# Chunk-selected attention with a gated FFN: FFN products in free order with the first eight in parts, masks as minimum or select, unit 3 by DMA transposes

## The chip, the cores and the metric

The kernel runs on one core of a Trainium2 chip. The core has five engines with a queue each: TensorE (PE), VectorE (DVE), ScalarE (ACT), GpSimd (POOL) and SyncE (SP, which here only issues DMAs). The metric is the device time of one launch in microseconds, the median over runs.

## The reference, cut to what matters

```
ub     = sum_d max(q * k_min[chunk], q * k_max[chunk])      # 24 chunks of 32 keys
top    = the 6 chunks of largest ub among the causal ones, for each query
scores = q @ k.T / 8, kept where the chunk is in top and the key is not after the query
attn   = softmax(scores) @ v                                # 4 batches, 8 heads, 768 rows, 64 wide
x      = attn with the heads side by side                   # 3072 x 512
out    = (sigmoid(x @ w_gate) * (x @ w_val)) @ w_out        # d_ff 1536
```

All inputs and the output are float32.

## The kernel before, in words

The 24 blocks of 128 query rows (4 batches of 6) are cut into eight units of three blocks. Unit 0 holds the first block of batches 0, 1 and 2 (and the first block of batch 3 goes with unit 2): there every causal chunk is among the six, so no choice is made, and `first` (L604) does all of it. Units 1 to 7 go through `prepare` (L1263: keys and queries turned and cast, `choose` at L789 for the bounds and the choice), `attend` (L847: scores, exponential, causal mask, product with v, division) and a feed-forward part: `ffn` (L937) for units 0 to 3, and `ffn_pair` (L1016) for 4 with 5 and 6 with 7, where seven products do the work of eight.

The causal part of the mask lies in the diagonal blocks. `attend` and `first` clear the upper triangle of the exponentials with an `affine_select` on POOL (L880 and L658). The chunk mask is added in the score product itself: half of the 128 contracted rows hold the key, the other half a fixed pattern of -60000 (`hkp`, L498, copied from `epat`) against a 0/1 choice of the query (`hqm`). Values arrive in float32 and are cast to half precision on POOL (`cast_v`, L576; for the first blocks `vc`, L642, on POOL or ACT).

`finish` (L910) divides by the sum and turns x so that the FFN can contract over it. For units below XBAR = 4 this is done by TensorE (`xps`, L931) with an eviction (`xT`, L933); from unit 4 on it is a DMA transpose issued by SP (L920).

`ffn` runs for each of 12 blocks of 128 FFN columns a gate product `g` (4 matmuls of 384 columns, L956), a tanh on ACT, a value product `v` (L962) and a gating on DVE (`hg`, L964), and then the product with w_out (`project_out`, L968), which `o0`, `o1`, `o2` take in thirds of the 12 blocks for each of three row blocks. All `g`, `v` and `o` name the key "ffn" as written, so that they keep the order of the code among themselves.

The order of all work is written out: `ORDER` (L97 to L283) is one list of 1982 names, and each engine's queue is that list filtered by engine. After a colon stand the buffer slots that an operation takes, after an @ the engine where it is not the first that the operation allows. Every engine runs its queue strictly in order, so an operation that waits holds all that stand behind it on its engine. `Plan.add` (L50) finds what an operation depends on. The cost figures in `act`, `dve`, `pool` and `pe` (L286 to L302) are the planner's and have no effect on the program.

`BEATS` (L95) are transposes of a constant on TensorE with no use for the result, 78 of them in 13 groups. They stand between the first operations of the list. Loads are issued by SP, the weights by POOL (`weights`, L515), which casts them on the way; these wait for the operations `after0` to `after6` (L510), each of which reads a word of an earlier load.

Of the kernel before, what the change touches and what calls it, by code (L numbers as in the profile page):

```python
# [15 lines left out]
XBAR = 4  # L16
# [78 lines left out]
BEATS = (20, 9, 8, 3, 3, 10, 5, 1, 2, 2, 6, 6, 3)  # L95

ORDER = """  # L97
ident k3_u1:0 kcr0 epat0:0 kf1_0:0 v10 k0_u1 epat q2_u1 kf0_0 q1_u1 q0_u2:1 hkp010 hkp001@ACT k2_u1 ap0 hkp011@POOL
q3_u2 kn_u1_3:0 q0_u1 beat0:7 kT_u1_3:0 qf1_0:1 after2 kn_u1_0@POOL:1 qf0_0 kT_u1_0:1 k1_u1 qn_u1_1@DVE:0 hkp000 q3_u1
qT_u1_1:2 kt_u1_0:0 hkp100@POOL ident16 vf_0:2 kx0_u1_3 qf_u1_1:0 kt_u1_3@DVE:1 ap1 k0_u2 qn_u1_0:0 qn_u2_0@DVE:1  # L100
qf1_1:3 qn_u1_2@DVE:2 kn_u1_2:3 beat1:7 qT_u1_0:2 after0 kx1_u1_0:0 hkp110@ACT qT_u2_0:3 kf0_1:4 hk0_u1_3 qfT_0:4
kfT_0:5 kn_u1_1@POOL:1 qf16_0@DVE:0 qf0_1 qn_u2_3:4 kx1_u1_3 qn_u1_3:5 after3 vf_2:0 kf16_0:6 kxf0 hk1_u1_3@ACT
beat2:7 scf_0:0,4,1 v16_0_0 kT_u1_2:6 qf_u1_0 vf_1:1 kn_u2_0:0 hk0_u1_0 kx0_u1_2 hq0_u1_1@POOL expf_0_0 beat3:7
kT_u2_0:2 qT_u1_2:7 qf_u2_0:1 kf1_1 cmf_0_0 kt_u1_2:1 expf_0_1:2 q2_u2 hk1_u1_0@POOL beat4:0 pvf_0_0:3 kT_u1_1:0
qm_u1_1@ACT:0 hq1_u1_1@DVE kf0_2:0 qT_u1_3:4 after1 kx0_u1_0 vf1_2:1 qf0_2:1 kxf1:1 vc_2@ACT after6 qf1_2 qm_u1_0@ACT
kcr_f kx1_u1_2 cmf_0_1 kf1_2 qf_u1_2 kx1_u2_0:1 qf_u1_3 v11 beat5:1 pvf_0_1:7 k3_u2 qfT_1:6 kx0_u1_1 after4
qm_u1_3@ACT after5 wg0 kfT_1:4 q1_u2 rzf_0_1:0 kt_u2_0@DVE:0 qf16_1:5 k2_u2 hk0_u2_0 wv0 kt_u1_1:2 kf16_1@DVE:2 k1_u2
vf1_1:0 wg1 qm_u1_2 v_0_2:4 beat6:1 scf_1:4,6,1 qn_u2_2@DVE:3 hkp111 expf_1_1:3 v_0_3:3 beat7:1 qT_u2_2:5 qfT_2:1 hq0
vc_1@ACT kx1_u1_1 cmf_1_1 kfT_2:6 expf_1_0 rzf_0_0:1 kcr_u1@POOL xf_0_0:0 qf16_2:3 kf16_2@DVE:2 cmf_1_0 beat8:0
xpsf_0_0:3,0 xTf_0_0@ACT hkf0@DVE wv1 beat9:0 scf_2:6,1,2 qf_u2_2 xf_0_1:0 pvf_1_0:3 hk0_u1_2@ACT ub_u1:4,0 kx0_u2_0  # L110
hq0_u2_2@POOL expf_2_0 wg2 kn_u2_3@DVE:2 expf_2_1:1 hq0_u1_2@DVE pvf_1_1:6 rzf_1_0:0 hq0_u1_3 xf_1_0:1 cmf_2_1
ubn1_u1:0 qn_u2_1:0 vf1_3:3 rzf_1_1:0 hq1_u1_3 cmf_2_0 xf_1_1:2 beat10:5 qT_u2_1:0 xpsf_0_1:3 hq1 pvf_2_1:1
hq1_u2_0@POOL ubn0_u1 xpsf_1_1:6 xTf_0_1@ACT pvf_2_0:2 xpsf_1_0:7 kT_u2_3:5 hq0_u2_0 wv2 rzf_2_0:0 rzf_2_1:1
hk1_u2_0@ACT kn_u2_2@DVE:2 xf_2_0:1 wo0 qf_u2_1 v_0_1:0 xf_2_1:2 xTf_1_0@ACT beat11:4 xpsf_2_0:2 xTf_1_1@ACT ubm0_u1
xpsf_2_1:7 hk0_u1_1@ACT kn_u2_1@DVE:1 kT_u2_2:1 qT_u2_3:6 hk1_u1_1@POOL xTf_2_0 beat12:4 kT_u2_1:0 xTf_2_1 kt_u2_2:0
mx0_u1:0 wo1 hkp101@ACT g_u0_0:7,0,0 ap0_u1 wo2 apt0_u1:0 kx0_u2_2 qf_u2_3 v_u0_0:2 hq0_u1_0 hqm0_u1_2@DVE
g_u0_1:6,1,1 hq0_u2_3@POOL kx1_u2_1 hq1_u2_2@POOL v_u0_1:4 hk1_u1_2@POOL tanh_u0_1 tanh_u0_0 g_u0_2:3,2,2 hqm0_u1_0
hg_u0_1 kt_u2_1:1 v_u0_2:7 kx1_u2_2 hk0_u2_1@POOL tanh_u0_2 hg_u0_0 sc_u1_2_0:1,0 g_u0_3:3,1,3 hg_u0_2 exp_u1_2_0
# [187 lines left out]
def kernel(  # L306
# [1079 lines left out]
```

## Time and profile before

| | |
|---|---|
| median of 3 runs | 285.58 us (285.08 to 287.19) |
| profiled execution, whole | 284.64 us |
| its span, first to last instruction | 282.9 us |
| mean granted TensorE clock | 0.994 |
| bytes moved by DMA | 34.28 MB |
| first FFN product of unit 0 | 31.05 us |

The page gives each engine's busy time, the span in 40 slices, DMA queues, the chain of waits and the costliest groups of instructions. A row of a group reads: line, engine, operation, output from input, shape, count, then busy us and mean ns of one, then the idle time just before it and what ended it. In rows of the timeline the first two numbers are the start and the length in us.

### The profile page before, as it was taken

What the parts mean: (1) busy time and instruction counts of PE and PEld (TensorE: products, weight loads), DVE (VectorE), ACT (ScalarE), POOL (GpSimd) and SP (SyncE); (2) the same over time, 40 slices, a digit from 0 to 9 for tenths busy, and PEclk for the clock granted to TensorE, in tenths of its full rate; (3) what the DMA queues carried; (4) which work ended last, traced back from release to release, by engine and by line L of the source; (5) the groups of instructions that cost most, each with busy time, mean ns of one, the idle gap of its engine ahead of it and who ended that gap; (6) DMA issues with size and microseconds to landing.
All of it is one profiled execution on the core that took longest, in us unless ns stands there. A gap on an engine that the chain in (4) does not pass through costs nothing.

```text
span 282.9 us, 7408 instructions
## 1 busy us (share of the span) xinstructions
PE 271.4 (96%) x2746; PEld 187.4 (66%) x2746; DVE 245.1 (87%) x665; ACT 215.5 (76%) x467; POOL 144.5 (51%) x221
## 2 busy tenths in 40 slices
PE   6998899999999999999999999999999999999994
PEld 5875565765666656754777666667666786676783
DVE  2788778529979999997998998999999999999983
ACT  4787897665667956877899998989999937778620
POOL 7468673245433765773567974415648310347020
PEclk9799999999999999999999999999999999999999
DMA  6999999999989999999920112200001013010005
GB/s 174 292 232 184 197 197 208 162 189 222 147 194 163 228 173 215 180 205 185 228 62 17 30 30 67 89 20 13 14 16 29 16 49 117 0 39 37 3 19 204
DMA packets 130035, 34.28 MB, mean 121 GB/s; under 512 B 118096, under 2 KB 127056, under 8 KB 130000
## 3 DMA queue, kind: packets, MB, share of 16 engines
q1 hardware_dynamic: 125248, 29.11, 48.9%
q0 software_dynamic: 4752, 4.72, 10.2%
q8 instruction: 21, 0.34, 0.5%
q14 instruction: 14, 0.11, 0.1%
HBM read 30.67 MB, written 6.29 MB: 131 GB/s over the span
## 4 chain that ended last, share of the span: by engine, by line
PE 77%; DVE 12%; ACT 5%; issue 3%; POOL 2%; POOLq 0%; DVEq 0%; ACTq 0%
PE g_u L952 11%; PE v_u L952 11%; PE sc_u L863 10%; PE o_u L983 8%; PE pv_u L896 6%; PE suo_u6u L1210 3%; PE suv_u6u L1069 3%; PE suo_u4u L1210 3%; PE sug_u6u L1069 2%; PE sug_u4u L1069 2%; PE suv_u4u L1069 2%; PE ube_u L801 2%; PE sro_u6u L1210 1%; PE sro_u4u L1210 1%; PE srv_u6u L1069 1%
## 5 line engine op out<-in xcount | busy, mean ns | idle before, releaser
L874 ACT ACTIVATE att_u<-sc_u 128x512 f16<-128x512 f32 (+3 forms) x184 | 90.6, 550 | 14.1 <-PE sc_u L863 13.0
L880 POOL TENSOR_SCALAR_AFFINE_SELECT att_u<-att_u 128x384 f16<-128x384 f16 (+1 forms) x56 | 29.0, 529 | 40.0 <-ACT att_u L874 34.8
L952 PE MATMUL g_u<-xT_u,wg 128*128 128x384 f16 x192 | 39.0, 326 | 1.0 <-DVE hg_u L964 0.6
L952 PE MATMUL v_u<-xT_u,wv 128*128 128x384 f16 x192 | 39.0, 326 | 0.0
L983 PE MATMUL o_u<-wo,hg_u 128*128 128x512 f16 x144 | 36.1, 379 | 0.0
L960 ACT ACTIVATE gate_u<-g_u 128x384 f16<-128x384 f32 x48 | 23.1, 494 | 12.3 <-PE g_u L952 10.6
L964 DVE SCALAR_TENSOR_TENSOR hg_u<-gate_u,v_u 128x384 f16<-128x384 f16 x48 | 25.2, 537 | 5.4 <-PE v_u L952 4.2
L896 PEld LDWEIGHTS <-att_u 128*128 128x128 f16 x640 | 25.3, 98 | 4.7 <-issue 0.2
L863 PE MATMUL sc_u<-hqo,hko 128*128 128x128 f16 (+2 forms) x220 | 27.9, 243 | 0.3 <-ACT att_u L874 0.2
L863 PE MATMUL sc_u<-hqe,hke 128*128 128x128 f16 (+2 forms) x220 | 27.4, 243 | 0.3 <-DVE ubn_u L812 0.3
L896 PE MATMUL pv_u<-v,att_u 128*128 128x65 f16 x640 | 27.6, 193 | 0.0
L952 PEld LDWEIGHTS <-wg 128*128 128x128 f16 x192 | 18.2, 98 | 11.9 <-issue 1.4
L952 PEld LDWEIGHTS <-wv 128*128 128x128 f16 x192 | 18.3, 98 | 11.1 <-DVE x_u L915 0.3
L863 PEld LDWEIGHTS <-hko 128*128 128x128 f16 x220 | 17.0, 98 | 7.3 <-issue 1.6
L863 PEld LDWEIGHTS <-hke 128*128 128x128 f16 x220 | 16.3, 98 | 7.5 <-issue 1.5
L983 PEld LDWEIGHTS <-hg_u 128*128 128x128 f16 x144 | 13.2, 98 | 10.5
L578 POOL CAST v<-v 128x512 f16<-128x512 f32 x23 | 14.8, 659 | 2.6 <-DMA v<-in_v_dram 2.1
L915 DVE TENSOR_TENSOR x_u<-pv_u,rz_u 128x384 f16<-128x384 f32 (+1 forms) x28 | 14.7, 528 | 0.6
L1192 POOL TENSOR_TENSOR v<-hgp_u 128x384 f16<-128x384 f16 x5 | 4.5, 914 | 20.3 <-PE suv_u6u L1069 13.7
L473 PE MATMUL beat<-ident 128*128 128x128 f32 x78 | 13.4, 322 | 1.4 <-POOL ident masks.py:199 1.4
L824 DVE MAX8 mx_u<-ubn_u 128x8 f32<-128x8 f32 (+16 forms) x152 | 12.7, 157 | 0.0
L473 PEld LDWEIGHTS beat<-ident 128*128 128x128 f32 x78 | 11.3, 169 | 1.7 <-POOL ident masks.py:199 1.4
(284 smaller groups left out, 695.6 us busy)
## 6 DMA issues: line engine op xcount, KB each, us to landing
v<-in_v_dram SPq DMA_DIRECT2D x23, 256.0 KB, 4.6
k<-in_k_dram SPq DMA_DIRECT2D x12, 384.0 KB, 6.4
q<-in_q_dram SPq DMA_DIRECT2D x12, 384.0 KB, 5.8
out_dram<-osb_u SPq DMA_DIRECT2D x16, 256.0 KB, 2.8
wg<-in_moe_w_gate_dram POOLq DMA_DIRECT2D x3, 512.0 KB, 13.8
wv<-in_moe_w_val_dram POOLq DMA_DIRECT2D x3, 512.0 KB, 13.8
wo<-in_moe_w_out_dram POOLq DMA_DIRECT2D x3, 512.0 KB, 20.7
out_dram<-osb_u6u SPq DMA_DIRECT2D x5, 256.0 KB, 2.0
```

What stands on the lines that cost most here:

```text
L473: nc.tensor.transpose(at(beat), ident32, ident32)
L578: plan.add(f"v16_{b}_{ib}", {POOL: pool(H * D)}, lambda e: nc.gpsimd.tensor_copy(v16[b % 2][:, ib, :, 0:D], at(t)), reads=[t], writes=[("v ...
L863: nc.tensor.matmul(at(t)[:, o:o + 128 * m], hk[b % 2][e_][:, p, 128 * jb:128 * jb + 128], hq[u.side][e_][:, p, 128 * x:128 * (x + m)], sta ...
L874: plan.add(f"exp_{u.name}_{h}_{y}", {ACT: act(n)}, lambda e, t=t, att=att, b0=b0, n=n: nc.scalar.activation(at(att)[:, b0:b0 + n], at(t), ...
L880: nc.gpsimd.affine_select(out=dv, in_=dv, compare_op=ALU.is_ge, fill=0.0, base=0, pattern=[[0, u.m], [1, 128]], channel_multiplier=-1)
L896: nc.tensor.matmul(at(pv)[:, last, x, :], at(att)[:, c:c + 128], v16[b % 2][:, jb, h, :], start=(jb == 0), stop=(jb == ib))
L952: nc.tensor.matmul(at(t), w16[:, c, 128 * fb:128 * fb + 128], at(u.xt)[:, c, :], start=(c == 0), stop=(c == 3))
L960: plan.add(f"tanh_{u.name}_{fb}", {ACT: act(T)}, lambda e, g=g, gate=gate: nc.scalar.activation(at(gate), at(g), AF.Tanh, scale=0.5), read ...
L964: plan.add(f"hg_{u.name}_{fb}", {DVE: dve(T)}, lambda e, w_=w_, gate=gate, hg=hg: nc.vector.scalar_tensor_tensor(at(hg), at(gate), 1.0, at ...
L983: nc.tensor.matmul(at(o), hgs[c][1][1]()[:, 128 * tb:128 * tb + 128], wo16[:, fc, lo:hi], start=(c == 0), stop=(c == NFB - 1))
L1069: nc.tensor.matmul(at(t), left[i](c), right[i](c), start=first and c == 0, stop=c == 1, skip_group_check=not first)
L1210: nc.tensor.matmul(at(t), sums[what[i][0], f][1]()[:, 128 * tb:128 * tb + 128], what[i][1](f), start=first and f == 0, stop=f == half - 1, ...
```

## The change

The diff without the new `ORDER`, which is a different list of 1999 names (of the operations in both, some 160 stand on another engine, and the order and the slots are new throughout):

```diff
-XBAR = 4
+XBAR = 3
-BEATS = (20, 9, 8, 3, 3, 10, 5, 1, 2, 2, 6, 6, 3)
+BEATS = (14, 9, 4, 3, 8, 1, 3, 2, 1, 10, 2, 1, 4, 2, 2, 4)
...
+    tri = lone("tri", [128, 128])
+    const("tri0", {DVE: (90, 160)}, lambda e: nc.vector.memset(tri, 65504.0), writes=["tri"], prio=-4)
+    const("tri", {POOL: (260, 300)}, lambda e: nc.gpsimd.affine_select(
+        out=tri, in_=tri, compare_op=ALU.is_ge, fill=0.0, base=0, pattern=[[1, 128]], channel_multiplier=-1),
+        reads=["tri"], writes=["tri"], prio=-3.5)
...
-                const(f"hkp{i}{e_}{o}", {DVE: dve(2 * S, 4, 64), POOL: pool(2 * S), ACT: act(2 * S, False, 64)},
...
+                for w, cols in enumerate((slice(0, 512), slice(512, S))):
+                    n = 2 * (cols.stop - cols.start)
+                    const(f"hk{'pq'[w]}{i}{e_}{o}", {DVE: dve(n, 4, 64), POOL: pool(n), ACT: act(n, False, 64)},
+                          lambda e, i=i, e_=e_, o=o, cols=cols: copy(e, hk[i][e_][MASK[e_], o::2, cols],
+                              hk[0][e_][MASK[e_], o::2, cols] if i else at(epat)[:, o].rearrange(
+                              "p c s -> p (c s)")[:, cols].unsqueeze(1).to_broadcast([64, NP // 2, cols.stop - cols.start])),
...
-        plan.add(f"v16_{b}_{ib}", {POOL: pool(H * D)}, lambda e: nc.gpsimd.tensor_copy(
-            v16[b % 2][:, ib, :, 0:D], at(t)), reads=[t], writes=[("v16", b % 2, ib)], prio=prio)
+        plan.add(f"v16_{b}_{ib}", {POOL: pool(H * D), DVE: dve(H * D, 1.8), ACT: act(H * D, False)}, lambda e: copy(
+            e, v16[b % 2][:, ib, :, 0:D], at(t)), reads=[t], writes=[("v16", b % 2, ib)], port=True, prio=prio)
...
-            plan.add(f"cmf_{b}_{e_}", {POOL: pool(512)}, lambda e, e_=e_: nc.gpsimd.affine_select(
+            plan.add(f"cmf_{b}_{e_}", {POOL: pool(512), DVE: dve(512, 2)}, lambda e, e_=e_: nc.gpsimd.affine_select(
                 out=at(att[e_]), in_=at(att[e_]), compare_op=ALU.is_ge, fill=0.0, base=0,
-                pattern=[[0, NP], [1, 128]], channel_multiplier=-1), reads=[att[e_]], writes=[att[e_]], prio=next_())
+                pattern=[[0, NP], [1, 128]], channel_multiplier=-1) if e == POOL else nc.vector.tensor_tensor(
+                at(att[e_]), at(att[e_]), tri.unsqueeze(1).to_broadcast([128, NP, 128]), ALU.min),
+                reads=[att[e_], "tri"], writes=[att[e_]], port=True, prio=next_())
...
+                        if e == DVE:
+                            nc.vector.tensor_tensor(dv, dv, tri.unsqueeze(1).to_broadcast([128, u.m, 128]), ALU.min)
+                            return
...
-            def product(t, w16, fb=fb):
+            def product(t, w16, fb=fb, lo=0, hi=T):
                 def emit(e):
                     for c in range(4):
-                        nc.tensor.matmul(at(t), w16[:, c, 128 * fb:128 * fb + 128], at(u.xt)[:, c, :],
+                        nc.tensor.matmul(at(t)[:, lo:hi], w16[:, c, 128 * fb:128 * fb + 128], at(u.xt)[:, c, lo:hi],
                                          start=(c == 0), stop=(c == 3))
...
-            op = plan.add(f"g_{u.name}_{fb}", pe(650), product(g, wg16), reads=xt + [("wg", fb // 4)], writes=[g, "ffn"],
-                          prio=next_())
...
+            early = u.i == 0 and fb < 4
+            parts = [("", 0, 256, xt[:0] + [(u.xt, c, x) for c in range(4) for x in range(2)]),
+                     ("b", 256, T, [(u.xt, c, 2) for c in range(4)])] if early else [("", 0, T, xt)]
+
+            for tag, lo, hi, need in parts:
+                op = plan.add(f"g{tag}_{u.name}_{fb}", pe(4 * ((hi - lo) / 2.4 + 2.5)), product(g, wg16, lo=lo, hi=hi),
+                              reads=need + [("wg", fb // 4)] + ([g] if lo else []), writes=[g], prio=next_())
...
-            plan.add(f"v_{u.name}_{fb}", pe(650), product(w_, wv16), reads=xt + [("wv", fb // 4)], writes=[w_, "ffn"],
-                     prio=next_())
+            for tag, lo, hi, need in parts:
+                plan.add(f"v{tag}_{u.name}_{fb}", pe(4 * ((hi - lo) / 2.4 + 2.5)), product(w_, wv16, lo=lo, hi=hi),
+                         reads=need + [("wv", fb // 4)] + ([w_] if lo else []), writes=[w_], prio=next_())
...
-        project_out(u, list(enumerate(hgs)), ["ffn"], next_)
+        project_out(u, list(enumerate(hgs)), [], next_)
```

What it does: the FFN products of units 0 to 3 no longer keep the order of the code (the key "ffn" is gone), and the new list names them in another order. For the first four FFN blocks of unit 0 each of the eight products is cut into columns 0 to 255, which need two of the unit's three blocks, and 256 to 383. A causal mask may be done on DVE as a minimum with `tri`, a tile that holds 65504 on and below the diagonal's side that is kept and 0 on the other; in the new list 15 masks are done so and 49 stay selects on POOL. Unit 3's x is turned by four DMA transposes. In the new list three value casts are on DVE, six on ACT and the others on POOL. The pattern copies come in two parts each, and the second copy of a pattern is taken from the first. The beats are 70 in 16 groups. The same values are computed.

More of the change, by code (lines that the diff above doesn't have):

```diff
@@ L102 @@
[L102 to L116, printed above, removed]
@@ L641, in first @@
                      writes=[val], prio=next_() - 0.2)
-            plan.add(f"vc_{b}", {POOL: pool(H * D), ACT: act(H * D, False)}, lambda e: copy(e, at(val)[:, :, 0:D], at(raw["v"])),
+            plan.add(f"vc_{b}", {POOL: pool(H * D), ACT: act(H * D, False), DVE: dve(H * D, 1.8)}, lambda e: copy(e, at(val)[:, :, 0:D], at(raw["v"])),
                      reads=[raw["v"]], writes=[val], prio=next_())
```

375 lines of the change are left out of this document (196 added, 179 removed).

## The prediction

> **What bounds the kernel now.** I read the page first, then busy time by stretch, then what TensorE waited for, then the chain of waits at the start, then single groups.
>
> ```profile
> span 282.9 us, 7408 instructions
> PE 271.4 (96%) x2746; PEld 187.4 (66%) x2746; DVE 245.1 (87%) x665; ACT 215.5 (76%) x467; POOL 144.5 (51%) x221
> ```
> ```profile
> 0.00:31.05 31.05, 25.54 (x234) 21.21 (x235) 22.13 (x68) 22.76 (x47) 22.11 (x46) 0.95 1.02 218
> 31.05:65.00 33.95, 33.61 (x319) 21.16 (x317) 21.53 (x79) 26.55 (x59) 16.20 (x30) 1.00 1.16 191
> 65.00:135.00 70.00, 69.04 (x707) 42.90 (x706) 64.72 (x172) 48.95 (x100) 38.15 (x58) 1.00 1.00 191
> 135.00:185.00 50.00, 49.27 (x633) 33.98 (x632) 47.62 (x158) 46.28 (x95) 34.00 (x49) 1.00 0.30 72
> 185.00:230.00 45.00, 44.72 (x495) 32.36 (x494) 43.98 (x97) 41.42 (x96) 20.93 (x26) 1.00 0.09 19
> 230.00:265.00 35.00, 34.91 (x241) 23.33 (x239) 33.25 (x71) 25.96 (x63) 11.12 (x12) 1.00 0.12 46
> 265.00:282.90 17.90, 14.30 (x130) 12.42 (x127) 11.89 (x28) 3.57 (x11) 1.95 (x2) 1.00 0.24 89
> ```
>
> The columns after each stretch are its length, then busy us of PE, weight loads, DVE, ACT and POOL, the granted clock, the DMA engines' busy share and GB/s. From 31.05 to 265 us PE is idle for 2.4 us out of 234. So the time is, nearly: the moment at which PE's steady work begins, plus the PE work that is left then, plus a tail of 3.6 us. What an edit does to DVE, ACT or POOL counts only if it moves that beginning or opens a hole. Two things stand close behind PE: DVE from 185 us on (43.98 of 45.00 us), and the DMA engines up to 135 us (share 1.00 and more).
>
> The beginning at 31.05 us is the first FFN product of unit 0:
>
> ```profile
> 29.40 0.55 ACT xT_u L357 x2
> ...
> 30.94 1.47 ACT hke L357
> ...
> 32.44 0.38 ACT qf_u L357
> ...
> 32.86 0.81 PE g_u L952 x4
> ```
> ```profile
> 31.05 0.81 PE L952 MATMUL g_u<-xT_u,wg 128*128 128x384 f16 x4
> 31.70 0.81 PE L952 MATMUL v_u<-xT_u,wv 128*128 128x384 f16 x4
> 32.86 0.81 PE L952 MATMUL g_u<-xT_u,wg 128*128 128x384 f16 x4 [0.34 <-ACT qf_u L357]
> ```
>
> Before it PE also runs 78 "beats", transposes of a constant that only fill holes. The chain of waits there passes from ACT to DVE to POOL and back: 22 to 23 us of work on each of three engines in 31 us, in the order of their queues. The start is bound by that order. The weights are not late: the first of them lands 8.9 us after its issue at 18.0.
>
> ```profile
> L517 POOL DMA_DIRECT2D wg<-in_moe_w_gate_dram x3: 742/770/1002, 18.0 to 24.3; - x3
> ...
> DMA to landing us min/median/max: 8.9/13.8/16.1
> ```
>
> **The change, part by part.** (1) *The start's new order.* I compared the two instruction orders up to the first FFN product (now a value product of columns 0 to 255 of block 2). PE has 66 beats ahead of it, not 78; POOL is relieved of unit 0's six masks. The eight pattern copies are now cut into parts of 512 and 256 columns, and two large and six small parts stand ahead, 10/3 of a copy in place of eight (the one at 30.94 above took 1.47 us on ACT). DVE has the six masks more, fewer key and query copies, and by count about the same sum up to the last division of x. What differs for DVE is when it begins:
>
> ```profile
> 3.66 0.38 DVE L492 MEMSET ap<- 128x384 uint32 x1
> 7.69 0.55 DVE L359 COPY qn_u<-kq_u 128x384 f32<-128x384 f32 x1 [3.66 <-PE kT_u L700]
> ...
> 29.14 0.74 DVE L673 TENSOR_TENSOR xf<-pvf,rzf 128x256 f16<-128x256 f32 x2
> ...
> 30.02 0.54 DVE L359 COPY xT_u<-xpsf 128x256 f16<-128x256 f16 x2
> ```
>
> The 3.66 us of idleness go if the data are there. In the new order a query copy is fourth in DVE's queue and its load is first on SP; with the 4.0 us from issue to landing that the loads of this kind have below it would begin near 5 us, 2.7 earlier. Against this, the loads of the third first block stand one place later on SP, about 0.5 us. The ends are 0 (the loads decide) and 3.7 (all of that hole). I take 1.5 us, the middle less a little for the loads: the first product at about 29.5.
>
> (2) *Products in free order, the first eight in parts.* 32 matmuls more, the same columns. A 384-column matmul takes 0.1625 us (four in 0.65 above), so 256 columns take about 0.108, and 128 take 0.055 (rows of part 3): 32 x 0.001, at most +0.1 us. In return the lower parts need only two of the three first blocks: ACT's last two evictions of x, 0.55 us in the chain above, lie beside the lower part of the first product (0.43 us). That is inside the 1.5. The value products come before the gate products and the first value weights are now issued first, so the weights stay hidden: with 8.9 us from 18 to 19 us they are there at 27 to 28.
>
> (3) *Unit 3 by DMA transposes.* Four groups of three PE transposes go, with four evictions (two each on ACT and DVE, about 0.49 us, off PE's path).
>
> ```profile
> L929 PE MATMUL xps_u<-ident,x_u 128*128 128x128 f16 x32 | 3.8, 219 | 0.2
> L357 ACT COPY xT_u<-xps_u 128x384 f16<-128x384 f16 x4 | 1.9, 487 | 1.3 <-PE xps_u L929 1.3
> ```
> ```profile
> v<-in_v_dram SPq DMA_DIRECT2D x23, 256.0 KB, 4.6
> kq_u<-in_k_dram SPq DMA_DIRECT2D x4, 192.0 KB, 4.0
> xT_u<-x_u SPq DMA_TRANSPOSE x8, 2.4
> ```
> ```profile
> 50.98 0.86 PE o_u L983 x4
> ```
> ```profile
> 55.29 0.33 PE L929 MATMUL xps_u<-ident,x_u 128*128 128x128 f16 x3
> 55.45 0.39 PE L863 MATMUL sc_u<-hqo,hko 128*128 128x128 f16 x4
> ```
>
> Start to start three transposes take 0.16 to 0.17 us: -0.7 us of PE for twelve. But the eight transposes of the trace ran after 148 us, where DMA is a third busy, and landed in 2.4 us. Unit 3's fall near 120 us, where it is full and a load of 256 KB takes 4.6. On PE, between the last attention product that the last of them needs and the first FFN product of unit 3, stand six thirds of unit 2's output rows (0.86 us each) and scores of 23 x 128 columns (0.055 each), 6.4 us. After sums on DVE (two gatings, one block transpose, reciprocal and division, some 2 us) 4.4 us are left: idle DMA would be early by 2, full DMA late by 0.2 to 1 with a load in front. SP also holds the loads behind each until x is ready; four such waits, the values of block 1 among the loads. I take +0.4, with ends 0 and 3.
>
> (4) *Masks as a minimum on DVE, or as selects on POOL.* Fifteen of 64 move (48 + 8 + 8 in the two rows below and their smaller form): unit 0's six, one of batch 3's first block, eight of the wide units.
>
> ```profile
> L880 POOL TENSOR_SCALAR_AFFINE_SELECT att_u<-att_u 128x384 f16<-128x384 f16 x48 | 25.6, 546 | 33.8 <-ACT att_u L874 29.0 <-issue 4.4
> L658 POOL TENSOR_SCALAR_AFFINE_SELECT attf<-attf 128x512 f16<-128x512 f16 x8 | 5.2, 649 | 7.1 <-ACT attf L656 7.1
> L1192 DVE TENSOR_TENSOR hgp_u<-hg_u,hgp_u 128x384 f16<-128x384 f16 x7 | 3.2, 452 | 0.0
> L578 POOL CAST v<-v 128x512 f16<-128x512 f32 x23 | 14.8, 659 | 2.6 <-DMA v<-in_v_dram 2.1
> L357 ACT CAST vf<-vf 128x512 f16<-128x512 f32 x3 | 1.9, 619 | 0.0
> ```
>
> No minimum is in the trace. The nearest row is DVE's half-precision sum at 0.45 us, so +7 us on DVE, ends 0.34 (its shortest) and 0.65 (POOL's select) each: 5 to 10 us. POOL loses 15 x 0.55 to 0.65, about 8.5 us. The six at the start are in part (1). By the new order most of the others stand between unit 0's last products and unit 1's first, 50 to 65 us, where the idle time is:
>
> ```profile
> 50.00:65.00 15.00, 15.00 (x171) 10.22 (x170) 6.73 (x20) 10.69 (x26) 5.96 (x11) 1.00 1.02 177
> ```
>
> DVE is busy for 6.73 of 15 us there, so eight masks (3.6 us) fit: 0 on the path. Had they stood after 185 us, where 1 us of 45 is free, they would have cost some 2.6 us.
>
> (5) *Value casts on any engine.* Six go to ACT, three to DVE: 0.62 us each there, 0.66 less on POOL. One of them shows what that is worth: while POOL cast four blocks of v in a row, a copy of 768 columns on DVE lasted 2.27 us; a maximum over 640 took 0.48 elsewhere.
>
> ```profile
> 94.97 2.27 DVE L359 CAST k<-k 128x768 f16<-128x768 f32 x1
> ```
> ```profile
> 95.10 2.61 POOL L578 CAST v<-v 128x512 f16<-128x512 f32 x4
> ```
> ```profile
> 86.54 0.48 DVE L602 TENSOR_SCALAR qm_u<-qf_u 128x640 f32<-128x640 f32 x1
> ```
>
> Some 1.7 us of DVE can come back there; PE's holes from 65 to 135 us are 1.0 in all. I take a third of the 1.7, -0.6, with ends 0 and 1.7. But a cast waits for its load, and what is queued behind it on ACT is exponentials, which hold PSUM banks. The cast of batch 2's last block comes on ACT only 2.1 us of PE work after the place of its load on SP, and the load takes 4.6. If SP runs no further ahead, ACT stands for 2.5 us; ACT is busy for 48.95 of 70 us there, so most is absorbed. I take +0.3, ends 0 and 2.5.
>
> The Trainium skill, "SBUF — State Buffer", Terms (shared port pair), has VectorE and GpSimd take one port pair in turn, a whole instruction at a time, the loser waiting; "GPSIMD Engine Reference", its table of specifications, counts VectorE instructions with two SBUF inputs among those that contend. The 2.27 us agree. By that rule the new minimum is held up by POOL too; that is rival E.
>
> **Sum.** Start -1.5; PE work left at the first product: -0.7 +0.1, and +0.2 for one transpose group of unit 2 that now comes after it; the four beats that now stand behind the first eight products (0.4) are set off by the hole of 0.5 at 32.86, which the old order had. Waits: +0.4 +0.3 -0.6. Together -1.8 us. The profiled execution took 284.64 us (282.9 and 1.7 around it), so 282.8; the median of the runs, 285.58, stands 0.9 above it, and on that scale it is 283.8.
>
> **Rivals.** A is this forecast, 282.5 to 285.3.
> B: the start gains the whole 3.7 us and DVE gets back the 1.7: with the other terms (-0.4 +0.4 +0.3) 285.58 - 5.1 = 280.5; with half of the surplus 282.1. For it: three engines lose work ahead of the beginning. Against it: 1.02 DMA share in that stretch.
> C, the other side: the last transpose of unit 3 waits behind loads on the full DMA. Its place is the first gate product of unit 3, near 128 us. It decides once it lands over 6.6 us after its issue, since that eats the 4.4 and the 2.2 of the other terms; at 9.2 us (two loads of 4.6 in front) PE stands 4.8 us: 285.58 - 2.2 + 4.8 = 288.2. For it: one queue. Against it: the loads of k and v before it mostly have slots early.
> D: the start comes earlier but the wide DMA stretch does not, and PE waits later for k1 and v: 285.4. For it: share 1.16 from 31 to 65. Against it: only one wait of 2.1 for v by POOL.
> E: each minimum waits for a running POOL instruction. At 0.6 us each the two of the third first block lie on the start's chain, +1.2, and the rest in idle time: 285.0.
>
> **How the numbers follow.** A 0.40, B 0.22, C 0.18, D 0.12, E 0.08. Predicted is A's 283.8. The range goes from 281.0, short of B's full 280.5, to 288.0, short of C's 288.2, and so leaves out about 2 in 10. Faster by over 1% (below 282.7; 1% is about what a measurement can tell) holds B and a little of A's low end, 0.29; slower by over 1% (above 288.4) holds C where the landing is as late as priced or later, and the casts' 2.5 us beside it, 0.18; within 1% 0.53. A's own range is 282.5 to 285.3.
>
> **What would show it.** Right: the first product at 28.5 to 30.5 us, PE idle below 3 us up to 265, no wait over 1 us of PE before unit 3's first product, the masks on DVE at 0.4 to 0.6 us, and no 2 us copy on DVE. Wrong: a first product at 31 or later (D, or E if the masks last 1 us); a hole on PE near 125 to 130 us with a transpose landing after 6 us or more (C); PE idle near zero and a first product before 28 (B). If DVE's or ACT's queue stands for v on DMA for over 1 us, part 5 was priced too low.

## The result and the profile after

The changed kernel takes 282.2 us, the median of 6 runs (280.6 to 288.8), beside 285.75 for the kernel before on the same chip: a ratio of 0.9846, interval 0.9815 to 0.9877. Run again (e5 below) it took 281.77 beside 285.64: 0.9855, interval 0.9821 to 0.9889. The highest of the six, 288.8, ran at a lower granted clock (0.987) and is left out of the ratio. So it is faster by 3.5 to 3.9 us between the medians, 1.2 to 1.4%, and by 1.5% (4.1 to 4.4 us) by the ratios, where 1.8 us were forecast. The profiled execution took 282.25 us with a span of 280.2, 2.7 less than the span before.

The first lines of its page, and then busy time of PE by stretch (length, busy us, granted clock, DMA share, GB/s), from its first FFN product on:

```profile
span 280.2 us, 7449 instructions
PE 268.8 (96%) x2758; PEld 186.3 (67%) x2758; DVE 246.8 (88%) x679; ACT 220.4 (79%) x474; POOL 134.6 (48%) x206
```
```profile
29.27:65.00 35.73, 35.69 (x366) 1.00 1.15 194
65.00:133.00 68.00, 66.35 (x688) 1.00 0.94 180
133.00:183.00 50.00, 49.95 (x640) 1.00 0.47 101
183.00:228.00 45.00, 44.84 (x493) 1.00 0.10 23
228.00:263.00 35.00, 34.89 (x238) 1.00 0.10 38
263.00:280.20 17.20, 13.80 (x126) 0.97 0.28 108
sum 250.93, PE 245.52; mean PE 40.92
```

The same view of before, from 31.05 us on, sums up to:

```profile
sum 251.85, PE 245.85; mean PE 40.97
```

Two things are to be seen. The steady work begins 1.78 us earlier. And the small holes of before are gone (0.04 us idle up to 65 us, 0.32 in the 130 us after 133), but for one of 1.65 us between 65 and 133. The first products, then the place of that hole, in SP's, DVE's, ACT's and PE's rows:

```profile
29.27 2.80 PE L968 MATMUL v_u<-xT_u,wv 128*128 128x256 f16 x32
31.91 0.61 PE L480 MATMUL beat<-ident 128*128 128x128 f32 x4
32.35 1.48 PE L968 MATMUL g_u<-xT_u,wg 128*128 128x256 f16 x16
```
```profile
113.09 4.18 SPq L936 DMA_TRANSPOSE xT_u<-x_u  x1
117.38 1.14 SPq L583 DMA_DIRECT2D v<-in_v_dram  x2
118.57 0.88 SPq L573 DMA_DIRECT2D k<-in_k_dram  x1
```
```profile
109.16 0.56 DVE L931 TENSOR_TENSOR x_u<-pv_u,rz_u 128x384 f16<-128x384 f32 x1
```
```profile
124.10 0.83 ACT L359 CAST k<-k 128x768 f16<-128x768 f32 x1 [3.03 <-DMA k<-in_k_dram]
124.94 0.83 ACT L359 COPY hqe<-apt_u 64x768 f16<-64x768 f16 x1
```
```profile
PE sc_u L876 <- ACT hqe L359: 1.2, 1, 1.2
PE sc_u L876 <- ACT att_u L887: 0.4, 1, 0.4
```

The second transpose of unit 3 occupies SP for 4.18 us. It does not wait for its input in that time: its x is ready at 109.72 us (the DVE row), 3.4 us before SP begins with it. The key load behind it is issued at 118.57, its cast on ACT stands 3.03 us, the choice's copy `hqe` stands behind the cast, and the scores wait for that copy. The transposes themselves were in time: none of PE's waits names one.

### The profile page after: what moved, and what is told of

It is laid out like the page before. It is cut to its first block, busy times and chain, and to the rows that moved or that the text cites. A ratio compares the mean times of both kernels' runs of the same rounds, so it can differ in the third digit from the quotient of the medians.

```text
span 280.2 us, 7449 instructions
## 1 busy us (share of the span) xinstructions
PE 268.8 (96%) x2758; PEld 186.3 (67%) x2758; DVE 246.8 (88%) x679; ACT 220.4 (79%) x474; POOL 134.6 (48%) x206
## 4 chain that ended last, share of the span: by engine, by line
PE 83%; DVE 5%; ACT 4%; DMA 3%; issue 2%; SPq 1%; POOL 0%; ACTq 0%; DVEq 0%
PE sc_u L876 12%; PE g_u L968 11%; PE v_u L968 10%; PE o_u L1006 10%; PE pv_u L912 6%; PE suo_u6u L1233 3%; PE suo_u4u L1233 3%; PE sug_u4u L1092 3%; PE suv_u4u L1092 3%; PE sug_u6u L1092 2%; PE suv_u6u L1092 2%; PE ube_u L814 2%; DMA k<-in_k_dram 2%; DMA kq_u<-in_q_dram 1%; PE sro_u4u L1233 1%
## 5 line engine op out<-in xcount | busy, mean ns | idle before, releaser
L896 POOL TENSOR_SCALAR_AFFINE_SELECT att_u<-att_u 128x384 f16<-128x384 f16 (+1 forms) x48 | 26.8, 570 | 44.0 <-ACT att_u L887 42.8
L968 PE MATMUL g_u<-xT_u,wg 128*128 128x384 f16 (+2 forms) x208 | 37.6, 314 | 0.0
L968 PE MATMUL v_u<-xT_u,wv 128*128 128x384 f16 (+2 forms) x208 | 36.4, 313 | 0.0
L1006 PE MATMUL o_u<-wo,hg_u 128*128 128x512 f16 x144 | 35.3, 379 | 0.1
L876 PE MATMUL sc_u<-hqe,hke 128*128 128x128 f16 (+2 forms) x220 | 28.2, 243 | 1.6 <-ACT hqe L359 1.2
L968 PEld LDWEIGHTS <-wv 128*128 128x128 f16 x208 | 19.1, 98 | 10.1 <-issue 0.5
L365 POOL CAST v<-v 128x512 f16<-128x512 f32 x15 | 9.1, 612 | 12.9 <-DMA v<-in_v_dram 9.4
L480 PE MATMUL beat<-ident 128*128 128x128 f32 x70 | 12.0, 305 | 1.4 <-POOL ident masks.py:199 1.4
L1092 PEld LDWEIGHTS <-Sg 128*128 128x128 f16 x96 | 9.0, 98 | 5.2
L1092 PEld LDWEIGHTS <-Sv 128*128 128x128 f16 x96 | 9.0, 98 | 5.0 <-issue 0.3
```

The source lines that it names most:

```text
L876: nc.tensor.matmul(at(t)[:, o:o + 128 * m], hk[b % 2][e_][:, p, 128 * jb:128 * jb + 128], hq[u.side][e_][:, p, 128 * x:128 * (x + m)], sta ...
L896: nc.gpsimd.affine_select(out=dv, in_=dv, compare_op=ALU.is_ge, fill=0.0, base=0, pattern=[[0, u.m], [1, 128]], channel_multiplier=-1)
L968: nc.tensor.matmul(at(t)[:, lo:hi], w16[:, c, 128 * fb:128 * fb + 128], at(u.xt)[:, c, lo:hi], start=(c == 0), stop=(c == 3))
L1006: nc.tensor.matmul(at(o), hgs[c][1][1]()[:, 128 * tb:128 * tb + 128], wo16[:, fc, lo:hi], start=(c == 0), stop=(c == NFB - 1))
L1092: nc.tensor.matmul(at(t), left[i](c), right[i](c), start=first and c == 0, stop=c == 1, skip_group_check=not first)
```

## The experiments

Most of them start from one edit, called the moved load here: the key load that stood behind the transpose goes ahead of it. All ratios are to the kernel before, run beside each kernel on the same chip.

### Before once more, and the moved load

e1 is the kernel before, unchanged.

> The kernel before, unchanged, once more with a profile. The prediction put the profiled execution 0.9 us below the median of the runs and carried that over to the changed kernel, where the profiled execution and the median agree (282.25 and 282.2). Theory S (the profiled execution of before was a lucky one): a new profiled execution lies at 285 to 286 us, span 283.3 to 284.2, and its extra time shows as holes of TensorE at a place that the first profile does not have. Rival R (profiling takes 1 us off this kernel): about 284.6 again, span 282.9, with no new hole.

Measured: 284.76 us, ratio 0.9994 (0.9970 to 1.0018); profiled 284.87, first product at 31.00. That is below S's 285 and 0.2 above the first profile, so neither theory is settled. Here the profiled execution lies at the median, 0.1 off. The medians of before beside the other kernels, in five measurements, are 285.0 to 285.75, so the distance to its two profiles (284.64, 284.87) is 0.1 to 1.1 us: its runs scatter upward (to 291.6), and no fixed amount stands between a profile and a median.

e2 is the moved load.

```diff
-... xT_u3_1 ... v_1_5 ... v_2_2 ... k01_3 ...
+... k01_3 xT_u3_1 ... v_1_5 ... v_2_2 ...
```

On SP the load so passes two value loads as well as the transpose.

> The changed kernel with one load (a quarter of batch 3's keys) put one place ahead on SyncE, before unit 3's second DMA transpose. Theory Q (that transpose holds SyncE for 4.2 us and so the load, which lands 1.6 us too late for ScalarE): the hole of 1.6 us of TensorE at 125 us is gone, 280.6 us. Rival: ScalarE is late there anyway, the hole stays over 1 us, 282 us.

Measured: 281.26 us, ratio 0.9870 (0.9840 to 0.9901). The hole is gone; the stretch that holds it and the sum from the first product on:

```profile
65.00:133.00 68.00, 68.00 (x701) 1.00 0.96 184
133.00:183.00 50.00, 49.94 (x637) 1.00 0.53 105
...
sum 249.16, PE 245.42; mean PE 40.90
```

That fits a load held behind the transpose, but one run does not show it: e5 below has the load in its old place and no hole either. And the ratio is no lower than the changed kernel's (0.9846), and the first product of this execution stood at 30.94 us although the start is the same. That asked for two things: how constant the start is, and how constant the hole.

### The two halves of the order

e3 takes before's order up to the first FFN product and the changed kernel's from there; e4 the changed kernel's start, and then before's order (products whole, unit 3 turned by TensorE).

```diff
-ORDER = start of after + rest of after
+ORDER = start of before + rest of after      # e3
+ORDER = start of after + rest of before      # e4, XBAR = 4
```

> The order of before up to the first FFN product, then the changed kernel's order, masks, casts and transposes. Theory M (the gain is the earlier start): first FFN product at 31.0 us and 1.8 us more than the changed kernel, 284.0. Rival P (the gain lies in the rest: masks and casts off GpSimd, free order): first product at 31.0 but the time stays below 283.

> The changed kernel's order up to the first FFN product, then the order of before (masks and casts on GpSimd, unit 3 turned on TensorE, whole products); what before did in its start and the new start does later (pattern copies, one transpose group of unit 2, some casts) stands ahead of the first product here, on its old engines. Theory M: first product at 29.5 to 30 us, 1 to 2 us less than before, 284. Rival P: 285.5, the start's gain is lost.

Measured: e3 286.86 us, ratio 1.0052 (1.0020 to 1.0084); e4 287.41, ratio 1.0098 (1.0060 to 1.0135). Each half alone loses. In e3 the first product waits 1.76 us for a copy that the new rest expects earlier, to 33.89 us, and behind that wait PE is slow: the first 32 matmuls take 4.46 us in place of 2.80, with the granted clock at 0.51 from 34 to 36 us. In e4 PE stands 3.9 us between 31 and 65 us. A start leaves work undone that its own rest takes up, so these two runs do not divide the gain.

### The start: TensorE at half its rate

e5 is the changed kernel again, e6 the moved load with ten beats more in PE's two waits of the start, e7 the kernel before with its waits filled.

```diff
-BEATS = (14, 9, ...)                 # e6
+BEATS = (14, 13, ..., 6)             # the last group behind the first key transposes
-BEATS = (20, 9, ...)                 # e7
+BEATS = (30, 9, ..., 6)
```

> The changed kernel as it is, once more. In its first profile the first FFN product began at 29.27 us and no transpose of the start took more than 0.55 us for a group of three; in the run with the key load moved, which has the same start, it began at 30.94 us, and three groups of transposes and nine beats between 6.9 and 10.6 us took 0.85 and 2.13 us where the first profile has 0.49 and 1.15. Theory K (the start has two lengths, 1.6 us apart, set by whether TensorE runs a stretch of about 3.4 us at half its rate): the first product stands near 29.3 or near 30.9 us and nowhere between, with the durations of the rows saying which. Theory F (the later start belonged to the moved load): 29.3 us again. Both: the hole of about 1.6 us at 125 us is there again, since the load behind the transposes is the same, and the median is 282.0 +- 0.6 us, a ratio of 0.984 to 0.990.

> The changed kernel with the key load moved ahead of the transpose (as in the second run) and with TensorE's two waits of the start filled: six beats more behind the first key transposes and thirteen in place of nine in the second group. Theory K: with no wait of 0.4 to 0.9 us before 8 us, TensorE does not drop to half its rate; groups of three transposes take 0.5 us all through the start, the first product stands at 29.5 us or earlier, and the median is 0.5 to 1.3 us under the 281.26 of the second run, a ratio of 0.982 to 0.986. Rival N: the beats change nothing but stand in the way of the transposes by up to 0.4 us; the first product stands at 30.9 to 31.3 in an execution with slow rows, and the ratio is 0.987 to 0.989.

> The kernel before with its waits of the start filled in the same manner: thirty beats in place of twenty at first (to 6.5 us, where TensorE stood 1.13 us), and six behind the first key transposes (where it stood 0.69 us); nothing else is changed. Theory K: the stretch at half rate from 8.4 to 11.8 us goes, the first product stands at 29.3 to 30.0 us in place of 31.0, and the median is 0.7 to 1.5 us lower, a ratio of 0.995 to 0.9975; then the start's new order by itself has earned next to nothing. Rival O (the start's gain was the new order of ScalarE, VectorE and GpSimd, and TensorE's rate there is hidden): the first product stays at 30.8 to 31.2 and the ratio is 0.999 to 1.002.

Measured: e5 281.77 us, ratio 0.9855 (0.9821 to 0.9889), first product at 30.28, and no hole at 125 us this time, against both theories. e6: 280.78, ratio 0.9853 (0.9818 to 0.9888), first product at 29.37. e7: 285.45, ratio 0.9994 (0.9972 to 1.0015), first product at 31.25. Three rows of PE in the first profile of the changed kernel, and the same three in e5:

```profile
5.76 0.77 PE L713 MATMUL qT_u<-ident,qn_u 128*128 128x128 f32 x3 [0.44 <-DVE qn_u L361]
6.36 1.15 PE L480 MATMUL beat<-ident 128*128 128x128 f32 x9
8.13 0.55 PE L713 MATMUL qT_u<-ident,qn_u 128*128 128x128 f32 x3 [0.62 <-DVE qn_u L361]
```
```profile
5.97 0.90 PE L713 MATMUL qT_u<-ident,qn_u 128*128 128x128 f32 x3 [0.64 <-DVE qn_u L361]
6.67 2.12 PE L480 MATMUL beat<-ident 128*128 128x128 f32 x9
8.59 0.84 PE L713 MATMUL qT_u<-ident,qn_u 128*128 128x128 f32 x3
```

The same nine beats take 1.15 us in one execution and 2.12 in another: up to about 6.2 us PE is slow in both, in e5 for some 3.6 us more, to 9.8. In the new start PE lies on the path at that point, and all that follows is shifted: at full rate (after, e6, and below e10, e11, e12, e15, e16) the first product comes at 28.96 to 29.37 us, with the longer slow stretch (e5, e2, e14) at 30.28 to 30.94. Theory K was right for the changed kernel, except that the later starts are 1.0 to 1.7 us later, not all 1.6. With the waits filled, the one profile of e6 shows full rate and its ratio lies in K's range, but it is no better than that of e5.

The hole at 125 us hangs on the start as well. In e5 the key load is issued at 118.73 us, as late as in the first profile, and ACT still waits 1.38 us for it; but PE comes there about 1 us later and does not wait. With the load moved and the first product at 29.0 to 29.4 us (e6, and below e11, e15, e16) PE is idle for 0.00 to 0.31 us from 65 to 133, beside 1.65 in the first profile. As far as these runs go, the hole needs both, the early start and the late load.

For the kernel before theory K fell, and rival O was right. Its profile has such a stretch from 8.4 to 11.8 us; e3, which has its start, ran at full rate there:

```profile
9.00 2.13 PE L473 MATMUL beat<-ident 128*128 128x128 f32 x9
...
20.32 0.40 PE L651 MATMUL scf<-qf,kf 64*128 64x128 f16 x8 [0.24 <-DVE kf L359]
```
```profile
8.25 1.15 PE L480 MATMUL beat<-ident 128*128 128x128 f32 x9
...
20.24 0.40 PE L662 MATMUL scf<-qf,kf 64*128 64x128 f16 x8 [0.24 <-DVE kf L361]
```

Behind the beats e3 is 1.7 us ahead (9.40 beside 11.13), at the scores 0.08: in the old order the waits for ACT, DVE and POOL cover PE's rate. So the new order gains 0.1 to 0.8 us with the longer slow stretch and 1.7 to 2.1 without it: it takes DVE's late beginning away, and then PE's rate is what is left.

The Trainium skill, "TensorE: Matmul & The Clock Gate", Part 1, has TensorE at half clock until a window of about 3.4 us has been busy, the window running freely, so that the number of slow matmuls changes from run to run. The rows agree: half the rate, for one stretch of about 3.5 us more in some executions. Its remark that the ramp is under 1% of a span holds too (1.6 us of 280), but that is as much as the start of this change was forecast to bring.

### One part undone at a time

Each of these has the moved load and undoes one part: e8 puts all masks on POOL, e9 the value casts on before's engines, e10 turns unit 3 by TensorE and evictions, e11 makes the first eight products whole, e12 puts the products of units 1 to 3 in the fixed order g, v, g, v.

```diff
-cmf_0_0@DVE ... cm_u1_2@DVE ...      # e8, 15 masks
+cmf_0_0 ... cm_u1_2 ...
-v16_0_0@ACT vc_1@DVE v16_0_3@DVE ... # e9, 11 casts
+v16_0_0 vc_1@ACT v16_0_3 ...
-XBAR = 3                             # e10, four xps and xT in place of four transposes
+XBAR = 4
-early = u.i == 0 and fb < 4          # e11, vb_u0_* and gb_u0_* leave ORDER
+early = False
-g_u1_4 g_u1_0 v_u1_3 g_u1_3 v_u1_4 ... # e12
+g_u1_0 v_u1_0 g_u1_1 v_u1_1 g_u1_2 ...
```

> The changed kernel with the key load moved, and all masks back on GpSimd as selects, at the same places of the order; 15 minima of 0.34 to 0.56 us leave VectorE, 15 selects of 0.52 us or more come to GpSimd. Theory M0 (as in the prediction: the masks lie beside other work, nothing on the path): the ratio is that of the second run, 0.985 to 0.989, and TensorE's idle time from the first product to 263 us stays under 0.8 us. Rival M1 (the minima earn, because six of them are the few-row unit's in the start, where GpSimd has the query and key copies to do): the first product comes 0.5 to 1.5 us later than its executions with the same TensorE rate give (29.3 or 30.9 us), TensorE waits in the first 20 us after it, and the ratio is 0.990 to 0.995.

> The changed kernel with the key load moved, and its value casts back on the engines that have them before: nine casts of 128x512 (0.41 us on VectorE, 0.63 on ScalarE) go to GpSimd (0.62), two of the first unit's go to ScalarE; their places in the order stay. Theory V0 (the casts lie beside other work, and GpSimd, 48% busy, has room): ratio 0.985 to 0.989 as in the run with the moved load alone, TensorE idle from the first product to 263 us under 0.8 us. Rival V1 (the casts are a good part of the small waits that went): GpSimd, which stood 14.8 us for value loads there, holds key and query copies behind a cast that waits for its load, and TensorE waits for a copy of GpSimd's; idle time 1.5 to 4 us, ratio 0.991 to 0.999.

> The changed kernel with the key load moved, and unit 3 turned by TensorE and evictions, as before, in place of the four DMA transposes: 12 transposes of 0.22 us come back to TensorE (about 0.7 to 1.4 us of its time), four evictions of 0.35 to 0.43 us to ScalarE and VectorE, and four transposes leave SP's queue. Theory P (as in the prediction: with the load no longer behind a transpose, what is left of this part is TensorE's saved 0.7 us): the time is 0.5 to 1.5 us more than with the moved load alone, ratio 0.989 to 0.9925. Rival Q (SP's queue is held by the transposes in other places as well, with loads late by what the profile does not show): no more or less, ratio 0.984 to 0.988, and GpSimd's waits for value loads between 90 and 130 us fall by several us.

> The changed kernel with the key load moved, and the first eight FFN products whole again (128x384 in one row) at the place of their first part. The third part of the queries is ready at about 29.1 us in the first profile, 0.2 us before the first product, so that the parts have next to nothing to cover. Theory N (parts are a small cost): TensorE issues 32 instructions less, worth 0.3 to 0.7 us (a pair of 272 and 219 ns in place of one of 326, pipelined), the first product moves by under 0.3 us, and the ratio is 0.983 to 0.987. Rival S (the parts let the start's end and the first products overlap): the first product is late by 0.5 us or more at an equal rate of the start's transposes, and the ratio is 0.988 to 0.991.

> The changed kernel with the key load moved, and in units 1 to 3 the products in the fixed order of before (g, v, g, v with the number of the product ascending) in the same places of TensorE's order; the tanh and the gating products stay in their places with their numbers sorted, four tanh moved behind the product that they read. The other work is not planned again for it. Theory F (the free order is what took TensorE's waits away, since scores and products that wait for VectorE or ScalarE stood behind a fixed pair before: 2.4 us idle from the first product to 265 us before, 0.4 us here): idle time of 2 to 5 us, the waits being of g or v for hg and of scores, ratio 0.993 to 1.003. Rival R (the order of the pairs is of no account, and the waits went with what else was planned anew, the copies, casts and masks of ScalarE, VectorE and GpSimd): idle time under 1 us, ratio 0.985 to 0.989.

| run | median us | ratio (interval) | first product | from there to the end |
|---|---|---|---|---|
| e2, moved load | 281.26 | 0.9870 (0.9840 to 0.9901) | 30.94 | 249.16 |
| e8, masks on POOL | 281.86 | 0.9886 (0.9844 to 0.9927) | 29.92 | 248.88 |
| e9, casts back | 285.60 | 1.0001 (0.9975 to 1.0027) | 34.86 | 249.94 |
| e10, unit 3 on PE | 281.64 | 0.9877 (0.9843 to 0.9910) | 28.96 | 249.74 |
| e11, no parts | 280.11 | 0.9838 (0.9794 to 0.9881) | 29.02 | 249.18 |
| e12, fixed order | 287.27 | 1.0063 (1.0044 to 1.0082) | 29.34 | 255.66 |

(The last column is the span of the profiled execution less the time of its first product.)

Masks, unit 3's transposes and parts are each worth less than the intervals. After the first product the masks cost or gain nothing (248.88 beside 249.16), as M0 had it. The first product of e8 is 0.55 us later than that of e6 at the same rate, as M1 had it (its ratio of 0.990 or more did not come): PE waits 0.9 us for a query load, and 0.82 us for a mask on POOL where in e6 it waits 0.49 for the same mask on DVE. Unit 3 on PE adds 0.4 (beside e6, 249.37) to 0.6 us there, near the low end of theory P, but the ratio lies in rival Q's range and its interval covers both; POOL's waits for value loads from 90 to 130 us fall only from 2.5 us (e2) to 0.7. Nothing speaks for a use of the parts (theory S of e11 is out; N's small gain is not resolved).

The free order is the one part without which larger waits come back after the first product. With pairs in fixed order PE stands in the units that changed, and the waits are those for ACT and DVE:

```profile
29.34:65.00 35.66, 35.62 (x365) 1.00 1.16 192
65.00:133.00 68.00, 65.88 (x682) 1.00 0.91 172
133.00:183.00 50.00, 47.34 (x616) 1.00 0.50 107
```
```profile
PE sc_u L877 <- ACT att_u L888: 2.1, 4, 0.8
PE v_u L969 <- ACT att_u L888: 1.1, 1, 1.1
PE v_u L969 <- ACT gate_u L983: 0.7, 2, 0.4
```

4.78 us idle in two stretches that have 0.06 in e2: theory F, though the ratio is higher than F's 1.003. (The sum is 6.5 us longer than e2's; the other 1.8 are busy time of PE, whose source was not traced.) It bounds the part from above only, since nothing else was planned anew for the fixed order. Before, with an order planned for fixed pairs, has 1.2 us idle in these two stretches.

e9 was a surprise in its place. The casts lose 4 us, all ahead of the first product; from there on (249.94) 0.8 us are lost at most. That is neither V0 nor V1.

### Which cast

e13 moves back only the first cast of unit 0's block 0 (to POOL), e14 only the one that goes from DVE to ACT, e15 only those after the first product. e16 is the moved load, the filled waits and whole products together.

```diff
-v16_0_0@ACT                          # e13
+v16_0_0
-vc_1@DVE                             # e14
+vc_1@ACT
-v16_0_3@DVE v16_0_2@DVE v16_0_5@ACT ... vc_3
+v16_0_3 v16_0_2 v16_0_5 ... vc_3@ACT # e15
```

> The changed kernel with the key load moved, and of the value casts only the first of unit 0's block 0 on GpSimd in place of ScalarE (0.62 us at about 17 us). Theory A (this cast delays GpSimd's guards ahead of the weight loads, and the last key load of the few-row unit comes in under the weights): the last kfT comes at 24 to 27 us in place of 22.0 to 23.4, the first product at 31.5 to 35 us, ratio 0.994 to 1.001. Theory B (the cast on ScalarE did it): the first product at 28.9 to 30.9 us, ratio 0.984 to 0.989.

> The changed kernel with the key load moved, and of the value casts only the second of the few-row unit's on ScalarE in place of VectorE (0.62 us at about 21 us). Theory B (ScalarE, which has no wait over 0.5 us from 14 to 22 us, is late by this cast with all that follows, the last key and value block among it): the first product 0.6 to 2 us later than in runs with the same rate of the first transposes (29.0 to 29.9 and 30.3 to 30.9 us), ratio 0.990 to 0.996. Theory A (the one on GpSimd): the first product as in those, ratio 0.984 to 0.989.

> The changed kernel with the key load moved, and only the value casts that come after the first FFN product back on the engines of before (eight to GpSimd, one to ScalarE). Theory S (all that the casts earn is earned ahead of the first product): ratio 0.984 to 0.989, TensorE idle from the first product to 263 us under 0.9 us. Rival V1 (they earn by small waits between products): idle 1.5 us or more, ratio 0.990 to 0.995.

> The changed kernel with the key load moved, TensorE's two waits of the start filled with ten beats more, and the first eight products whole. If the gains add up (the filled start by the rate, the parts' 32 instructions): median 279.8 to 280.6 us in the scale of the runs before, ratio 0.981 to 0.9835, spread of its runs under 1 us, first product at 29.0 to 29.6 us. If the filled start is worth nothing beside the rest: as without parts alone, ratio 0.9835 to 0.985.

Measured: e13 283.28 us, ratio 0.9910 (0.9876 to 0.9944), first product at 33.05. e14: 281.54, 0.9847 (0.9816 to 0.9878), 30.55, with the half-rate stretch. e15: 281.56, 0.9860 (0.9838 to 0.9882), 29.23. The late casts leave the ratio where it was, as theory S had it; PE's idle time from the first product to 263 us is 1.36 us, above S's 0.9 and below V1's 1.5, so that a part of a microsecond may be theirs. Ahead of the first product theory A has the right cast, and its times for the keys and the first product hold (its ratio of 0.994 or more does not). Its reason does not hold: POOL's last guard ends earlier than in e15, not later. Rows of e13 (the issue of the last key load of the few-row unit on SP, the first weight load on POOL, the transpose that uses the keys), then the same of e15:

```profile
18.21 1.71 SPq L552 DMA_DIRECT2D kf<-in_k_dram  x1
18.71 1.19 POOL L529 DMA_DIRECT2D wv<-in_moe_w_val_dram  x1 [0.36 <-issue]
25.90 1.09 PE L625 MATMUL kfT<-ident,kf 128*128 128x128 f32 x4 [3.48 <-DMA kf<-in_k_dram]
```
```profile
18.10 0.47 SPq L552 DMA_DIRECT2D kf<-in_k_dram  x1
19.08 1.06 POOL L529 DMA_DIRECT2D wv<-in_moe_w_val_dram  x1 [0.37 <-issue]
22.40 0.63 PE L625 MATMUL kfT<-ident,kf 128*128 128x128 f32 x4
```

With the cast on POOL the key load takes 1.71 us to issue and 7.6 to land; in the 2 us from 20 on the DMA engines move 47 GB/s beside 176 in e15:

```profile
20.00:22.00 2.00, 2.00 (x3) 1.00 0.53 47
```
```profile
20.00:22.00 2.00, 2.00 (x4) 1.00 0.92 176
```

PE stands 3.48 us, and the transpose after that wait takes 1.09 us in place of 0.63: the granted clock is 0.50 from 26 to 28 us (in e9, after a wait of 2.79 us, from 26 to 30). From that transpose to the first product e13 then takes 7.15 us beside 6.83 in e15, so most of the loss is the wait. The runs of e13 spread from 280.4 to 284.0, so this probably happens in some executions and not in others. A long issue beside the first weight load is not peculiar to this cast: the two loads behind, keys of unit 2, take 1.94 us to issue in the changed kernel (1.82 in e5, 2.17 in e2, 1.80 in e16) and 1.02 in e6 and e15. In e13 and e9 it meets the load that PE waits for. Why a cast of 0.62 us at 15.4 has this effect stays open: the weight load that overlaps the issue of the key load comes only 0.37 us earlier than in e15, and in e6 it came 0.40 us after that issue began without harm.

e16: 281.44 us, 0.9871 (0.9849 to 0.9894), first product at 29.33. The gains do not add up; no version was measurably better than the changed kernel, and the lowest, e11, overlaps it.

## Why the prediction was right or wrong

**The bound** held: PE is 96% busy after as before, and the time is its beginning, its work and a tail.

**Start, forecast -1.5.** -1.78 in one profile, -0.77 in the other. The forecast of 29.5 us for the first product lies between. The reason given, the hole of DVE before 7.69 us, was right: DVE's first copy of queries begins at 3.31 us (3.36 in e5). That TensorE's rate, hidden before, would then lie on the path was not seen.

**From the first product on, forecast -0.3 (-0.4 of PE's work, +0.1 of waits).** Measured -0.92 with the hole and -2.33 without (e5, 249.52). This is the step that failed: the +0.1 for PE's waits. Of the 2.33, 0.53 is PE's busy time (245.85 to 245.32), so the work was priced well. The other 1.80 is idle time, 6.00 to 4.20. The prediction had seen these waits: "From 31.05 to 265 us PE is idle for 2.4 us out of 234". It then let 0.5 of it go (the hole at 32.86) and 0.6 by way of the casts, and put 0.4 and 0.3 of new waits and 0.4 of beats in their place. Waits of before that are in neither profile of the changed kernel:

```profile
PE g_u L952 <- DVE hg_u L964: 0.6, 1, 0.6
PE sc_u L863 <- DVE ubn_u L812: 0.3, 1, 0.3
PE suv_u4u L1069 <- DVE c0g_u4u L1084: 0.3, 1, 0.3
PE sug_u4u L1069 <- DVE c0g_u4u L1084: 0.2, 1, 0.2
```

Of the 1.80 us, 1.05 lie between 65 and 183 us, where units 1 to 3 have their products, 0.58 between 183 and 228, and the rest in the tail. Part 2 priced the free order by its first eight products alone; what it does in units 1 to 3 has no term. Of these 1.80 it can stand for 1.05 at most: the last two rows are of the pair of units 4 and 5, whose products had no "ffn" key before either. How much is the free order and how much the rest of the new list stays open, since e12 takes the free order out of a list that was made for it. An edit counts, the prediction said, if it "moves that beginning or opens a hole"; one that closes holes counts too.

**Parts, +0.1.** Not contradicted; e11's ratio is lower, with an interval that overlaps.

**Unit 3, -0.7 and +0.4.** The work saved is 0.4 to 0.6 us (e10). The +0.4 lies between the hole of 1.65 in one profile and none in the other; that is luck, for the reason given is not what held the late load. "SP also holds the loads behind each until x is ready" is true of the third transpose and the fourth (in the first profile SP stands 1.2 and 0.7 us before them). Behind the second, x was long ready, and its issue itself took 4.18 us. Plain loads were slow to issue there too: two key loads took 4.09 us at 104.17. The mechanism of rival C, a late transpose, did not occur.

**Masks, 0.** On DVE they took 0.54 and 0.35 us in the mean (forecast 0.34 to 0.65), and after the first product all lie beside other work. In the start rival E's mechanism shows at the place that E names: the two minima of the third first block take 1.63 us together, from 24.90 on, where one takes 0.41 elsewhere, while POOL casts from 25.08 to 26.25. It is the same in e5, e6, e11 and e16. That is 0.8 us in place of E's 1.2, and PE waits 0.49 us for them:

```profile
26.58 0.30 PE L678 MATMUL pvf<-vf,attf 128*128 128x65 f16 x4 [0.49 <-DVE attf L671]
```
```profile
L671 DVE TENSOR_TENSOR attf<-attf,tri 128x512 f16<-128x512 f16 x7 | 3.6, 540 | 0.6 <-ACT attf L667 0.6
L894 DVE TENSOR_TENSOR att_u<-att_u,tri 128x384 f16<-128x384 f16 x6 | 2.0, 354 | 1.2 <-ACT att_u L887 1.2
```

**Casts, -0.6 and +0.3.** After the first product they are about right: without them PE has 0.4 (e9) to 1.0 us (e15) more of idle time than e2, too little for the medians. The copy of 768 columns that took 2.27 us is gone (0.88 at most now). Missed was the one cast of the start that on POOL costs some 3.8 us in the new order (e13's profile beside e15's); against before that is no gain, since there the same cast stands on POOL without harm.

**The scale, +0.9.** The forecast shifted the profiled 282.8 to the median 283.8. In the changed kernel the profiles, 282.25 and 281.82, lie at the medians, 282.2 and 281.77; each had either the hole or the longer slow stretch, and its fastest runs are 280.6 and 280.2. In before the distance is 0.1 to 1.1. So the profiles differ by 2.4 to 3.1 us, the medians by 3.5 to 3.9 and the ratios by 4.1 to 4.4: about 1 us of the measured gain may be scatter, and the +0.9 rested on three runs. The profiled execution is also longer than its span by 2.0 us now, by 1.7 before; the forecast kept 1.7.

Rival B's 282.1 came out for other reasons than B's: the start did not gain 3.7, and no run shows a gain from DVE's copy. A hole of a third of C's price came, from a late load. D did not occur, and E in part, under another sum. The bounds of A and D's 285.4 stand without a working; 283.8 without the start's 1.5 would be 285.3. The range, 281.0 to 288.0, held.

## What to carry to other kernels

When an order is written anew, the small waits of the bounding engine are part of the price list: sum them, and ask for each whether the new freedom lets other work stand in its place. A DMA transpose whose issue takes long holds the loads behind it on its queue, even when its input is ready; look there for the loss, and not only at the landing of the transpose. And before crediting one part with a gain at the start, look at two profiles of the same kernel: here the same order began its steady work at 29.3 and at 30.3 us.

## What the runs showed of the hardware

- TensorE ran at half rate for some 3.5 us within the first 12 us of some executions and not of others of the same program (nine beats in 1.15 or 2.12 us). In before the granted clock shows it (0.50 from 9 to 11 us); in e5 and e2 the clock column stands at 1.00 while the durations are doubled. The durations are the surer sign.
- After waits of PE of 1.76 (e3), 2.79 (e9) and 3.48 us (e13) within the first 35 us the granted clock read 0.50 or 0.51 for the next 2 us at least.
- The issue of a DMA transpose on SP took 1.2 to 4.18 us in the changed kernel, with x ready when it began.
- A minimum of 128x512 on DVE took 0.41 to 0.43 us in five places, and two in a row took 1.63 us together while POOL cast.
- The issue of one DMA on SP took 1.71 us (e13; 1.78 in e9) in place of 0.47 while GpSimd issued a weight load, and in e13 the DMA engines fell to 47 GB/s for 2 us although loads were pending. It was not settled what decides when this happens.
